# Plain-attention v as one stretch, key blocks of 128 under 160 queries, and half-height transposes in a windowed attention with a gated unit

## The chip, the cores and the metric

The kernel runs on one core of a Trainium2 chip. The metric is the device time of one launch in microseconds (us). The engines are TensorE (PE, matmuls; PEld is its weight loading), VectorE (DVE), ScalarE (ACT), GpSimd (POOL) and SyncE (SP), which here issues nearly all transfers.

## The reference, cut to what matters

```
q, k, v: (batch 8, heads 8, seq 576, head_dim 64), float32
rel = pos[:, None] - pos[None, :]
mask_plain = (rel >= 0) & (rel < 32)                        # heads 0 to 3
mask_dil   = (rel >= 0) & (rel < 128) & (rel % 4 == 0)      # heads 4 to 7
attn = softmax(where(mask, q @ k.T / 8, -1e9));  y = attn @ v
x = y, heads side by side: (8, 576, 512)
gate = sigmoid(causal depthwise convolution of x over 5 positions)
out = (gate * (x @ w_val)) @ w_out                          # (8, 576, 512) float32
```

Each query sees 32 keys: its own and the 31 before it (plain), or every fourth key of the last 128 (dilated).

## The kernel before, in words

A *unit* is four heads of one batch: the plain ones (0 to 3) or the dilated ones (4 to 7), so there are 16 units. In each batch but the last the dilated unit comes first. Per unit:

- `load_q` brings q and k as 128 partitions x 1152 values (576 KB each). v comes by `load_vd` (dilated: 80 and 112 partitions of 4 KB, 320 and 448 KB, overlapping in 48 rows of keys) or by `load_vp` (plain: two transfers of 64 partitions x 12 runs of 512 bytes, 384 KB each; the halves and blocks of 96 queries overlap by 32 keys).
- GpSimd casts the plain q and k to bf16 (`cvq`, `cvk`), and v (`cv`, line 325: dilated into `vd`, plain into `vpb`).
- `transposes` (line 469): 9 full 128x128 transposes for q and for k, into PSUM; `evict_t` copies them to `qT` and `kT` in two halves.
- `scores` (line 488): keys times queries. A plain task handles the even or the odd keys of two heads in blocks of 64 keys by 96 queries, 12 matmuls on 64x64 tiles of the array; a plain unit has four. A dilated task has 8 matmuls of 64 rows by 128 keys.
- `exps` (line 508, ACT) and `masks` (line 514, VectorE): 128 x 576 elements each, four per unit.
- `attn_p` (line 552): 24 matmuls of 64 rows and 65 columns (the 65th column of v is ones, and gives the softmax sum), two tasks per plain unit; `attn_d` (line 525) for the dilated units, into the same PSUM pair as its scores. `norm_p` and `norm_d` divide by the sum.
- `transpose_xp` (line 589: 12 of 96 columns per plain unit) and `transpose_xd` (line 573), and their evictions, write `xT`, a ring of three batches.

Per batch, once `xT` is complete: `conv` (line 607, 20 matmuls on 64x64 tiles for each of four channel chunks), `tanh` (ACT), `val` (line 622, 8 matmuls of 288 columns for each chunk) and `gate` (line 631, VectorE). The output: 36 tasks `outs` (line 638, 4 matmuls of 512 columns), `out_copy` into one of six `osb` buffers (line 643) and `store`.

The order of all this is made by the kernel's own planner when it is built. Each step is a `Task` with a key, a price in us for each engine that can take it, its dependences, its PSUM need (a *pair* of banks, a single *bank*, or a *score* pair, of which `SP` may be held at once) and, on PE, a shape class `cfg`: `F` full, `R` two row halves, `Q` quarters. `Plan` picks, at each step, among the tasks that can start within a slack of the earliest, the one with the lowest key; `KEY["W"]` is added for PE tasks of another shape than the current one, and `SWITCH` to their start. Where PE would stand idle early on, `fill` puts matmuls of `warm` (line 666). Transfers are issued by SP in one chain (`lane`), limited by `QUEUED` us of transfers on their way. The weights follow the loads of the unit that `WV` and `WO` name: units 0 and 1. The constants (identities, masks, `diag` for the convolution) are made mostly by GpSimd.

Of the kernel before, what the change touches and what calls it, by code (L numbers as in the profile page):

```python
# [1 line left out]

# [8 lines left out]
ALU = mybir.AluOpType  # L11


def hi_bf16(ap: bass.AP) -> bass.AP:
# [5 lines left out]
KEY = {"L": 171.6, "cv": -104.8, "T": -8.3, "ET": -139.2, "S": -21.7, "X": -137.2, "M": -69.8, "A": -31.3,  # L20
       "N": -35.2, "XT": 3.1, "XE": -124.1, "C": -15.3, "H": -46.4, "V": -4.0, "G": -205.2, "O":
       33.0, "P": -86.6, "SP": 2, "W": 10.4, "WV": 0, "WO": 1}


class Task:


    def __init__(self, name, key, opts, emit, deps=(), cfg=None, need=None,
                 frees=(), load=0.0, port=(), after=None, mm=0):
        self.name, self.key, self.opts, self.emit = name, key, opts, emit  # L30
        self.deps = [d for d in deps if d is not None]
        self.cfg, self.need, self.load, self.port = cfg, need, load, port
        self.frees = [f for f in frees if f is not None]
        self.after, self.mm = after, mm
        self.holders = 0
        for f in self.frees:
            f.holders += 1
        self.fin = None
        self.slot = None


class Plan:
# [6 lines left out]
    FETCH = 1.3  # L49
# [7 lines left out]
    def __init__(self, pairs, score_pairs):  # L57
# [6 lines left out]
        self.dma = 0.0  # L64
# [28 lines left out]
    def start_of(self, t, eng):  # L93
        s = self.free_at[eng]
        if eng == "PE" and t.cfg != self.cfg and self.cfg is not None:
            s += self.SWITCH
# [22 lines left out]
    def last_out(self, s, n):  # L119

        ahead = 0.0
        for d in reversed(self.queue[:n]):
            if d.start <= s:
                ahead += d.load
                if ahead > self.QUEUED:
                    return d
# [8 lines left out]
    def commit(self, t, eng, s):  # L135
# [5 lines left out]
        if t.load:  # L141
            self.dma = max(self.dma, s + (0.9 if t.name[0] == "s" else 2.4 if t.name[0] == "v" else 3.0)) + t.load
            t.fin = self.dma + 0.1
            if eng == "SP":
                t.start = s
                self.queue = sorted(self.queue + [t], key=lambda d: d.start)
        if eng in t.port:
            self.port[eng] = s + lat
        if eng == "PE":
            n = (self.mm + self.AHEAD) // self.LINE  # L150
            self.mm += t.mm
            for n in range(n + 1, (self.mm + self.AHEAD) // self.LINE + 1):
                self.dma = max(self.dma, s + 0.5) + self.FETCH
                self.lines[n + 1] = self.dma + 0.3
# [33 lines left out]
    def run(self):  # L188
# [12 lines left out]
        while ready:  # L201
            best = None
            for eng in self.free_at:
# [6 lines left out]
                s, k, t = min((x for x in c if x[0] <= s0 + self.SLACK[eng]), key=lambda x: (  # L210
# [11 lines left out]
        for n, t in enumerate(self.queue):  # L222
# [6 lines left out]
def kernel(  # L229
# [19 lines left out]
    QB = TT // 2  # L249
    KB = (80, 128)  # L250
    T1 = TT - KB[1]
    Z1 = 16
# [3 lines left out]
    NG = S // 192  # L256
# [5 lines left out]
    ETW = 400  # L262
# [7 lines left out]
    NVD, NQ, NE, NO = 3, 3, 6, 6  # L270
# [5 lines left out]
    qTs = [consts.tile([128, 2 * S], BF16, name=f"qT{i}") for i in range(2)]  # L276
    ets = [consts.tile([128, 2, ETW], BF16, name=f"et{i}") for i in range(NE)]
    vps = [consts.tile([128, 4 * NG, 2, D], FP32, name=f"vp{i}") for i in range(2)]
# [4 lines left out]
    vpb = [consts.tile([128, 2, 2 * NG, DA], BF16, name=f"vpb{i}") for i in range(NVD)]  # L283
# [4 lines left out]
    xnd = [consts.tile([QB, 8, 2, D], BF16, name=f"xnd{i}") for i in range(2)]  # L288
    xnp = [consts.tile([96, 2, NG, 2, 2, D], BF16, name=f"xnp{i}") for i in range(2)]
# [7 lines left out]
    ident_f = consts.tile([8, 8], FP32, name="ident_f")  # L297
    mask_d = consts.tile([128, HALF], BF16, name="mask_d")
    mask_p = consts.tile([128, 2, HALF], BF16, name="mask_p")
# [14 lines left out]

    def flat(ap):
# [12 lines left out]
    def band(dst, base, pattern, step):  # L328
        nc.gpsimd.affine_select(out=dst, in_=dst, compare_op=ALU.is_ge, fill=0.0,
                                base=base, pattern=pattern, channel_multiplier=-step)  # L330
        nc.gpsimd.affine_select(out=dst, in_=dst, compare_op=ALU.is_ge, fill=0.0,
                                base=W - 1 - base, pattern=[[-a, n] for a, n in pattern],
                                channel_multiplier=step)

    def eye(dst, n):
        nc.gpsimd.memset(dst, 0.0)
        nc.gpsimd.affine_select(
            out=dst, in_=dst, compare_op=ALU.not_equal, fill=1.0,
            base=0, pattern=[[-1, n]], channel_multiplier=1)

    def const(name, eng, dur, emit, deps=(), key=-50):
        return plan.add(name, key, {eng: (dur, dur + 0.05)}, lambda t: emit(), deps,
                        port=("POOL",))

    c_warm = const("warm0", "DVE", 0.5, lambda: nc.vector.memset(warm, 0.0), key=-60)  # L345
    c_eye = const("eye", "POOL", 1.0, lambda: eye(ident_b, 128), key=-60)
# [4 lines left out]
    c_sw = const("swap", "DVE", 0.25, swapped_eye, deps=[c_eye], key=5)  # L351

    def dil_mask():
        nc.gpsimd.memset(mask_d, 1.0)
        for z in range(2):
            band(mask_d[:, 2 * QB * z:2 * QB * (z + 1)].rearrange("p (h t) -> p h t", h=2),
                 z * (QB - T1), [[0, 2], [1, QB]], 1)

    c_md = const("mask_d", "POOL", 1.6, dil_mask, key=-57)

    def dil_ones():
        for x in vds[0] + vds[1] + vpb:
            nc.gpsimd.memset(x[:, :, :, D:DA], 1.0)
    c_vd = const("ones_d", "POOL", 0.4, dil_ones, key=-56)

    def small_eyes():
        eye(ident_f, 8)
        eye(ident_2[0:64], D)
        nc.gpsimd.tensor_copy(ident_2[64:128], ident_2[0:64])
    c_id = const("eyes", "POOL", 0.9, small_eyes, key=-55)  # L370

    def plain_mask():
        nc.gpsimd.memset(mask_p, 1.0)
        for s in range(2):
            m = mask_p[0:64, s, 0:96]
            nc.gpsimd.affine_select(out=m, in_=m, compare_op=ALU.is_ge, fill=0.0,
                                    base=W - s, pattern=[[1, 96]], channel_multiplier=-2)
            nc.gpsimd.affine_select(out=m, in_=m, compare_op=ALU.is_ge, fill=0.0,
                                    base=s - 1, pattern=[[-1, 96]], channel_multiplier=2)
        for g in range(1, NG):  # L380
            nc.gpsimd.tensor_copy(mask_p[0:64, :, 96 * g:96 * g + 96], mask_p[0:64, :, 0:96])
        nc.gpsimd.tensor_copy(mask_p[64:128], mask_p[0:64])
        nc.gpsimd.memset(mask_p[0:W // 2, :, 0:96], 0.0)
    c_mp = const("mask_p", "POOL", 2.6, plain_mask, key=-10)

    def dve_consts():
        for x in kTs:
            nc.vector.memset(x[:, 0:W], 0.0)
            nc.vector.memset(x[:, W + 2 * S:], 0.0)
        for x in ets:  # L390
            nc.vector.memset(x[:, :, HALF:], 1.0)
        nc.vector.memset(xT[:, :, :, 0:K - 1], 0.0)
        nc.vector.memset(vps[0][0:W // 2, 0], 0.0)
        for x in vas[1]:
            nc.vector.memset(x[0:Z1], 0.0)
    c_dv = const("dve_consts", "DVE", 2.2, dve_consts, key=-59)
# [8 lines left out]
    def dma(name, key, load, emit, deps=(), eng="SP", lane=None):  # L405
        def go(t):
            t.ins = emit()
            if getattr(t, "behind", None):
# [5 lines left out]
                     after=lane and lane[0])  # L414
# [19 lines left out]
    def load_vd(u, n, z):  # L434
        b = units[u][0]
        rows = v[b, 4:8].rearrange("h (p r) d -> p h (r d)", r=R)
        if z == 0:
            return [nc.sync.dma_start(out=vas[z][n % 2], in_=rows[0:KB[0]])]
        return [nc.sync.dma_start(out=vas[z][n % 2][Z1:KB[1]], in_=rows[T1 + Z1:TT])]

    def load_vp(u, n, half):
        b = units[u][0]
        dst = vps[n % 2][64 * half:64 * half + 64]
        first = v.offset + (b * H * S + 96 * half - W) * D
        skip = 1 if b == 0 and half == 0 else 0
        ins = []
        if skip:
            ins.append(nc.sync.dma_start(
                out=vps[n % 2][W // 2:64, 0].rearrange("p s d -> p (s d)"),
                in_=bass.AP(tensor=v.tensor, offset=v.offset,  # L450
                            ap=[[2 * D, 64 - W // 2], [1, 2 * D]])))
        ins.append(nc.sync.dma_start(
            out=dst[:, skip:].rearrange("p n s d -> p n (s d)"),
            in_=bass.AP(tensor=v.tensor, offset=first + skip * 192 * D,
                        ap=[[2 * D, 64], [192 * D, 4 * NG - skip], [1, 2 * D]])))
        return ins
# [4 lines left out]
    def transposes(t, u, name):  # L461
        d = units[u][1]
        if d:
            src = (qns if name == "q" else kns)[u % NQ]
        else:
            src = (qcs if name == "q" else kcs)[(u // 2) % 2]
        ps = pair(t).bitcast(BF16)
        for j in range(JP):
            nc.tensor.transpose(  # L469
                out=ps[:, j * 128:(j + 1) * 128],  # L470
                in_=hi_bf16(src)[:, j * 128:(j + 1) * 128] if d else flat(src[:, j]),
                identity=ident_b)

    def evict_t(t, tr, u, name, half):
        dst = kTs[u % 2][:, W:W + 2 * S] if name == "k" else qTs[u % 2]
        pv = pair(tr).bitcast(BF16)[:, 0:JP * 128].rearrange("p (j a) -> p a j", j=JP)
        dv = dst.rearrange("p (a j) -> p a j", j=JP)
        a = slice(64 * half, 64 * half + 64)
        copy(t, dv[:, a], pv[:, a])

    def scores(t, i, hf):
# [10 lines left out]
        if units[u][1]:  # L492
            for z in range(2):
                for hh in range(2):
                    o = (2 * e + hh) * 2 * TT + hf
                    for x in range(2):
                        mm(0, 128, (2 * z + hh) * QB, QB, x, W + o + 2 * z * T1, 2,
# [428 lines left out]
```

## Time and profile before

| what | value |
|---|---|
| three runs | 186.19, 186.78, 186.88 us; median 186.78 |
| the profiled execution | 189.71 us, of which the span of its instructions is 188.0 |
| mean granted clock of TensorE | 0.984 |
| transfers | 43.41 MB, mean 231 GB/s |
| fill matmuls of line 666 | 15.08 us of PE's busy time |
| Exp, 128 x 576 | 64 times, mean 654 ns |
| GpSimd idle, waiting for dilated v / plain v / k | 35.3 / 18.2 / 15.7 us |

The page is one execution taken by the hardware profiler. Its busy shares are means over the span; a stretch of the span can be asked for by itself, and so can the chain of waits that ended last, which is followed back from the last instruction. A group's row gives its line, engine, operation, tiles and shape, then the busy time and the mean of one in ns, then the idle time before it with what ended it. Matmuls are pipelined, so a group's mean is a latency and not the time that it takes from the next.

### The profile page before, as it was taken

The page shows a single profiled execution, that of the slowest core. Times are in us where ns is not written, and L with a number is a line of the kernel's source. Part 1 is how long each engine was busy: PE and PEld are TensorE (multiplying, and loading weights), DVE is VectorE, ACT ScalarE, POOL GpSimd, SP SyncE. Part 2 cuts the span into 40 slices and gives each one's busy share as a digit, 9 for nine tenths or more (in the row PEclk, how much of TensorE's full clock was granted, in tenths as well). Part 3 has the DMA queues.
Part 4 walks back from the last instruction along what each step waited for, and adds up shares of the span by engine and source line. Part 5 has one row for each costly group of instructions (what it writes and reads, how often), then busy time and mean ns, then how long its engine had stood idle before and what let it go on. Part 6 is the DMA issues. An engine that isn't in the chain of part 4 may idle for free.

```text
span 188.0 us, 6710 instructions
## 1 busy us (share of the span) xinstructions
PE 165.5 (88%) x2872; PEld 112.4 (60%) x2896; DVE 120.7 (64%) x233; ACT 124.3 (66%) x210; POOL 62.5 (33%) x99
## 2 busy tenths in 40 slices
PE   7988898998998999987998999789998999989930
PEld 2535455775685667664676677647676567557410
DVE  7498484795688858872877677567785488605000
ACT  2446799568775958684587846988777766672260
POOL 7974307325430723035153540711543230000000
PEclk9999999999999999996999999999999999999997
DMA  5999999899989988996799999859987840143265
GB/s 196 281 391 233 388 267 283 237 265 273 255 232 323 293 193 241 240 279 163 204 318 267 275 308 245 194 190 231 348 202 234 231 167 3 59 152 127 67 210 170
DMA packets 32102, 43.41 MB, mean 231 GB/s; under 512 B 1877, under 2 KB 20293, under 8 KB 32074
## 3 DMA queue, kind: packets, MB, share of 16 engines
q1 hardware_dynamic: 32064, 42.99, 80.7%
q8 instruction: 22, 0.36, 0.9%
q14 instruction: 6, 0.05, 0.1%
q10 hardware_dynamic: 10, 0.01, 0.0%
HBM read 33.56 MB, written 9.44 MB: 229 GB/s over the span
## 4 chain that ended last, share of the span: by engine, by line
PE 54%; DVE 12%; DMA 11%; ACT 11%; issue 6%; SPq 1%; ACTq 1%
PE ps L622 14%; PE ps L638 12%; PE ps L607 8%; PE ps L488 5%; PE ps L469 5%; DMA va<-in_v_dram 4%; ACT et L508 3%; DMA kn<-in_k_dram 3%; DVE et L514 3%; ACT osb L643 3%; DMA wst<-in_moe_w_out_dram 3%; PE ps L552 3%; PE ps L525 3%; DVE xnd L535 2%; PE ps L573 2%
## 5 line engine op out<-in xcount | busy, mean ns | idle before, releaser
L508 ACT ACTIVATE et<-ps 128x576 bf16<-128x576 f32 x64 | 40.6, 654 | 15.8 <-PE ps L488 14.6
L638 PE MATMUL ps<-w_out,gy 128*128 128x512 bf16 x125 | 34.0, 384 | 3.7 <-ACT osb L643 1.5
L622 PE MATMUL ps<-xT,w_val 128*128 128x288 bf16 x256 | 36.1, 287 | 0.6 <-DVE et L514 0.2
L325 POOL CAST vd<-va 80x512 bf16<-80x512 f32 (+1 forms) x32 | 19.3, 632 | 44.8 <-DMA va<-in_v_dram 35.3
L643 ACT ACTIVATE osb<-ps 128x512 f32<-128x512 f32 x36 | 20.8, 604 | 17.4 <-PE ps L638 11.4
L631 DVE SCALAR_TENSOR_TENSOR gy<-gy,ps 128x576 bf16<-128x576 bf16 x32 | 24.0, 750 | 12.6 <-PE ps L622 12.3
L622 PEld LDWEIGHTS <-w_val 128*128 128x128 bf16 x256 | 23.5, 97 | 8.3 <-issue 1.6
L607 PE MATMUL ps<-xT,diag 64*64 64x288 bf16 x640 | 24.6, 286 | 2.7 <-issue 1.8
L514 DVE TENSOR_TENSOR et<-et,mask_d 128x576 bf16<-128x576 bf16 x32 | 20.3, 640 | 8.7 <-ACT et L508 8.5
L615 ACT ACTIVATE gy<-ps 128x576 bf16<-128x576 f32 x32 | 20.4, 657 | 5.1 <-PE ps L607 4.6
L535 DVE TENSOR_TENSOR xnd<-ps,rec 72x512 bf16<-72x512 f32 x32 | 22.0, 687 | 1.1
L638 PEld LDWEIGHTS <-gy 128*128 128x128 bf16 x144 | 13.1, 99 | 15.5 <-issue 4.4
L325 POOL CAST vpb<-vp 128x768 bf16<-128x768 f32 x16 | 14.5, 935 | 22.3 <-DMA vp<-in_v_dram 18.2
L607 PEld LDWEIGHTS <-diag 64*64 64x64 bf16 x640 | 17.1, 106 | 6.7 <-issue 4.6
L488 PE MATMUL ps<-qT,kT 64*64 64x96 bf16 (+1 forms) x640 | 18.5, 205 | 1.8 <-ACT kT L323 1.1
L323 ACT COPY qT<-ps 128x576 bf16<-128x576 bf16 x26 | 15.7, 642 | 6.4 <-PE ps L469 5.6
L514 DVE TENSOR_TENSOR et<-et,mask_p 128x576 bf16<-128x576 bf16 x32 | 15.3, 493 | 6.0 <-ACT et L508 5.6
L488 PEld LDWEIGHTS <-kT 64*64 64x64 bf16 (+1 forms) x640 | 11.5, 102 | 12.8 <-issue 9.0
L323 ACT COPY kT<-ps 128x576 bf16<-128x576 bf16 x24 | 14.6, 646 | 4.1 <-PE ps L469 2.1
L666 PE MATMUL ps<-warm 128*128 128x512 bf16 x52 | 15.1, 415 | 2.4 <-DVE warm L345 1.3
L325 POOL CAST kc<-kn 128x1152 bf16<-128x1152 f32 x8 | 10.7, 1340 | 15.7 <-DMA kn<-in_k_dram 15.7
L323 ACT COPY xT<-ps 128x576 bf16<-128x576 bf16 (+1 forms) x19 | 13.6, 723 | 3.2 <-PE ps L638 2.0
(67 smaller groups left out, 179.2 us busy)
## 6 DMA issues: line engine op xcount, KB each, us to landing
qn<-in_q_dram SPq DMA_DIRECT2D x16, 576.0 KB, 5.4
kn<-in_k_dram SPq DMA_DIRECT2D x16, 576.0 KB, 6.9
out_dram<-osb SPq DMA_DIRECT2D x24, 256.0 KB, 3.2
vp<-in_v_dram SPq DMA_DIRECT2D x15, 384.0 KB, 6.0
va<-in_v_dram SPq DMA_DIRECT2D x8, 448.0 KB, 7.8
va<-in_v_dram SPq DMA_DIRECT2D x8, 320.0 KB, 7.0
out_dram<-osb SPq DMA_DIRECT2D x8, 192.0 KB, 2.3
wst<-in_moe_w_val_dram SPq DMA_DIRECT2D x2, 512.0 KB, 5.9
```

The source lines that it names most:

```text
L323: nc.scalar.copy(out=dst, in_=src)
L325: op(t.eng).tensor_copy(dst, src)
L488: nc.tensor.matmul(out=ps[po:po + pn, x, out_c:out_c + ln], lhsT=kw[rb, k0:k0 + (pn - 1) * kstep + 1:kstep], rhs=qT[rb, q0:q0 + (ln - 1) * ...
L508: nc.scalar.activation(out=ets[(2 * i + hf) % NE][:, :, 0:HALF], in_=ps[:, :, 0:HALF], func=AF.Exp, scale=scale)
L514: op(t.eng).tensor_tensor(out=ev, in0=ev, in1=m.to_broadcast([128, 2, HALF]), op=ALU.mult)
L535: nc.vector.tensor_tensor(out=xnd[i % 2][:, 4 * hf:4 * hf + 4].rearrange("p (x j) h d -> p x (j h) d", x=2), in0=av[:, :, :, 0:D], in1=rec ...
L607: nc.tensor.matmul(out=ps[o:o + 64, 512 * f:512 * f + HALF], lhsT=diag[lo:lo + 64, c * K + kk, :], rhs=xT[lo:lo + 64, b % NX, c, f * HALF ...
L615: nc.scalar.activation(out=gy[:, c, :, b, :], in_=ps[:, :, 0:HALF], func=AF.Tanh, scale=0.5)
L622: nc.tensor.matmul(out=ps[:, 512 * f:512 * f + HALF], lhsT=w_val[f][:, mc, c * 128:(c + 1) * 128], rhs=xT[:, b % NX, mc, K - 1 + f * HALF: ...
L631: nc.vector.scalar_tensor_tensor(out=y, in0=y, scalar=1.0, in1=ps[:, :, 0:HALF], op0=ALU.add, op1=ALU.mult)
L638: nc.tensor.matmul(out=ps, lhsT=y[:, c, 128 * n:128 * n + 128], rhs=w_out[f][:, c, :], start=(c == 0), stop=(c == NCH - 1))
L643: nc.scalar.activation(out=osb[z % NO], in_=bank(ou), func=AF.Copy, scale=0.5)
```

## The change

The plain v is loaded as one contiguous stretch of four heads: 1152 pairs of keys over 128 partitions, 9 pairs to a partition, in one transfer. The plain scores take two heads as one sequence of 18 blocks of 64 even and 64 odd keys (9 blocks a head), each seen by 160 queries: the 128 of its own positions and the 32 after. They go into three score tasks per unit instead of four, each 128 x 960, with their own Exp, mask and buffers (`etp`). The plain attention sums per block of 128 queries: two tasks of 35 matmuls. Its output transposes use column halves (class `Y`), 20 of 128 columns. The q and k transposes work on the two row halves (class `R`), 18 of 64 columns for each. The dilated v is loaded without overlap (80 and 64 partitions), and 32 of its rows are cast a second time into the second block; the dilated query blocks become 80 and 64 instead of 72 and 72, and the dilated attention takes a PSUM pair of its own. Masks, identities and `diag` are built mostly by VectorE. The planner gets a model of three transfer lanes, an order key for late outputs (`OB`), a tunable slack, new prices and new keys: w_val now follows unit 1 and w_out unit 2 (`WV` 1, `WO` 2), and three score pairs may be held.

```diff
-KEY = {"L": 171.6, ... "SP": 2, "W": 10.4, "WV": 0, "WO": 1}
+KEY = {"L": 336.6, ... "SP": 3, "W": -90.3, "WV": 1, "WO": 2, "OB": -5.9, "LOW": 0, "SL": 5.3}
...
-                s, k, t = min((x for x in c if x[0] <= s0 + self.SLACK[eng]), key=lambda x: (
+                s, k, t = min((x for x in c if x[0] <= s0 + (0.02 * KEY["SL"] if eng == "PE" else self.SLACK[eng])), key=lambda x: (
...
     def load_vd(u, n, z):
-        if z == 0:
-            return [nc.sync.dma_start(out=vas[z][n % 2], in_=rows[0:KB[0]])]
-        return [nc.sync.dma_start(out=vas[z][n % 2][Z1:KB[1]], in_=rows[T1 + Z1:TT])]
+        o = QB[0] * z
+        return [nc.sync.dma_start(out=vas[z][n % 2][o - T0[z]:o - T0[z] + QB[z]],
+                                  in_=rows[o:o + QB[z]])]
...
+    def load_vp(u, n):
+        b = units[u][0]
+        return [nc.sync.dma_start(
+            out=vps[n % 2].rearrange("p n s d -> p n (s d)"),
+            in_=bass.AP(tensor=v.tensor, offset=v.offset + b * H * S * D,
+                        ap=[[2 * D, 128], [256 * D, NP], [1, 2 * D]]))]
...
     def transposes(t, u, name):
         for j in range(JP):
-            nc.tensor.transpose(
-                out=ps[:, j * 128:(j + 1) * 128],
-                in_=hi_bf16(src)[:, j * 128:(j + 1) * 128] if d else flat(src[:, j]),
-                identity=ident_b)
+            for h in range(2):
+                a = slice(64 * h, 64 * h + 64)
+                ps = pair(t)[:, 512 * h:512 * h + 512].bitcast(BF16)
+                nc.tensor.transpose(out=ps[:, j * 64:(j + 1) * 64],
+                                    in_=src[a, j * 128:(j + 1) * 128], identity=ident_b[a, a])
...
+    def scores_p(t, u, g):
+        todo = [(n, x, half, x, 0, 64) for n in range(3) for half in range(2) for x in range(2)
+                if P_SLOT[g][x][n][0] != 4 or half == x]
+        if g == 2:
+            todo += [(2, x, 1 - x, 1 - x, p, 32) for p in (0, 32) for x in (1, 0)]
+        for n, bk, half, x, p, ln in todo:
+            nc.tensor.matmul(
+                out=ps[64 * half + p:64 * half + p + ln, c:c + QP],
+                lhsT=kw[rb, W + o + 2 * p + e:W + o + 2 * p + e + 2 * ln - 1:2],
+                rhs=qT[rb, o:o + QP], start=True, stop=True)
...
+    def attn_p(t, u, n, x):
+        for k in ks:
+            mm(k, 0, k, 0, 128, False)
+        mm(10 if x else 7, 0, 8 if x else 9, 0, 128, False)
+        for s in range(2):
+            for k in ks[:-1]:
+                mm(k, s, k + 1, 128, W, False)
+        for k in ks:
+            mm(k, 1, k, 0, 128, k >= ks[-2])
...
     def transpose_xp(t, u):
+            for n in range(5):
+                for e in range(2):
+                    nc.tensor.transpose(out=ps[64 * e:64 * e + 64, o:o + 128],
+                                        in_=xn[:, k % 2, k // 2 - 4 * x], identity=ident_b)
...
-    T_DG = add("diag", 4, {"POOL": (2.4, 2.5)}, lambda t: nc.gpsimd.tensor_tensor(
+    T_DG = add("diag", 4, {"DVE": (1.40, 1.45)}, lambda t: nc.vector.tensor_tensor(
...
-            TQ[u] = add(f"T{name}{u}", j0 + KEY["T"], {"PE": (0.50, 0.67)},
-                        [L[u] if d else C[u], c_eye], cfg="F", need="pair", mm=JP)
+            TQ[u] = [add(f"T{name}{u}", j0 + KEY["T"], {"PE": (0.31, 0.48)},
+                         (L[u] if d else [C[u]]) + dep + [c_eye], cfg="R", need="pair", mm=2 * JP)]
...
+                a = add(f"A{u}p{x}", j + KEY["A"], {"PE": (0.66, 0.83)},
+                        last + cvp[u][0:x + 1], cfg="R", need="pair", mm=35)
```

## The prediction

> **What bounds the kernel now.** I read the busy shares first, then the chain of waits, then the busy time by stretch, because a mean over the whole span hides that this kernel has three stages.
>
> ```profile
> PE 165.5 (88%) x2872; PEld 112.4 (60%) x2896; DVE 120.7 (64%) x233; ACT 124.3 (66%) x210; POOL 62.5 (33%) x99
> PE 54%; DVE 12%; DMA 11%; ACT 11%; issue 6%; SPq 1%; ACTq 1%
> ```
>
> TensorE (PE) is busiest and holds most of the chain that ended last. But 15.08 us of its 165.5 are the fill matmuls of line 666, which only keep it running: useful PE time is about 150 us. By stretch (columns: stretch, length, PE, PEld, DVE, ACT, POOL busy, clock, DMA share, GB/s):
>
> ```profile
> 0.00:30.00 30.00, 25.76 (x355) 14.50 (x361) 20.96 (x46) 18.62 (x30) 16.36 (x46) 1.00 0.99 293
> 30.00:150.00 120.00, 110.75 (x2185) 79.89 (x2200) 85.12 (x161) 87.58 (x150) 44.26 (x52) 0.99 0.92 251
> 150.00:180.50 30.50, 28.95 (x333) 17.99 (x336) 14.64 (x27) 15.88 (x27) 1.90 (x3) 1.00 0.30 98
> 180.50:188.00 7.50, 0.00 (x0) 0.00 (x0) 0.00 (x0) 2.26 (x5) 0.00 (x0) 0.82 0.60 204
> ```
>
> In the first 30 us the transfers run at 0.99 and 293 GB/s, and 14.48 of PE's 25.76 us are fills: the start is bound by loading. From 30 to 150 us PE is 92% busy and the transfers 92%: two limits lie side by side. After 150 us the loads are over and PE alone counts. After the last matmul, 7.5 us of copies and stores remain. The chain in order of time shows what the start waits for (columns: start, length, what):
>
> ```profile
> 2.28 7.35 DMA va<-in_v_dram
> 9.71 6.38 DMA kn<-in_k_dram
> 16.16 5.50 DMA wst<-in_moe_w_out_dram
> ...
> 33.25 0.98 PE ps L622 x8
> ```
>
> Three transfers in a row, the last one w_out, which no matmul needs until batch 0 is gated. The first value matmul starts at 33.25. Here the plain unit's k lands at 16.1 (9.71 + 6.38), behind q, k, v of unit 0 and the whole of w_val.
>
> **What the Trainium skill says.** "TensorEngine Tiling (Array Packing)", Key Properties: tiles of one mode load weights and multiply in parallel, and a change of mode drains the array. The trace agrees with both: the 24 plain attention matmuls of half height take 0.47 us in the chain, 19.6 ns each for 65 columns; and among 214 neighbouring pairs of groups in PE's timeline after 30 us, those of one shape overlap by 0.16 us, those of different shape (128 pairs) by 0.07, so a change costs 0.09 us. "SBUF — State Buffer", Who interferes with whom: a VectorE operation with two SBUF inputs and a GpSimd one that reads SBUF exclude each other. The trace agrees: the mask product has a median of 452 ns and a maximum of 3471 ns, in the start beside GpSimd's `diag` (2.32 us from 7.96). "ScalarE: Activation LUTs", What ACT_TABLE_LOAD costs: 186 ns + 0.833 ns per element for immediate scale and bias, 666 ns for 576 elements; measured 654.
>
> **The change part by part.** Durations are of the profiled execution: its own time is 189.71 us for a span of 188.0, against a median of 186.78. Some 2 us of the excess is one place, 83.8 us, where PE stands for 1.78 us at a dip of the clock (0.83 in 80 to 90 us). So I sum differences and apply them to the median.
>
> ```profile
> L488 PE MATMUL ps<-qT,kT 64*64 64x96 bf16 x384 | 9.4, 210 | 1.4 <-ACT kT L323 1.1 <-issue 0.3
> L552 PE MATMUL ps<-vpb,et 64*128 64x65 bf16 x384 | 9.0, 191 | 0.4 <-ACT et L508 0.4
> L589 PE MATMUL ps<-ident_b,xnp 96*128 96x96 bf16 x96 | 5.9, 216 | 0.1
> L469 PE MATMUL ps<-ident_b,qc 128*128 128x128 bf16 x72 | 5.3, 220 | 0.0
> ```
>
> The means are latencies of overlapped instructions; for a task's price I use its piece in the chain.
>
> 1. q/k transposes, 32 tasks: 9 full ones take 0.50 us; now 18 of half height and 64 columns. Nearest row: L552's 19.6 ns, so 18 x 19.6 = 0.35. Saving 0.15 x 32 = 4.7 us. Bounds: 0 if the halves don't overlap, 6 us if the planner's new price (0.31 for 0.50) is right.
> 2. Plain attention: 48 matmuls per unit become 70. 2 x 35 x 19.6 ns = 1.37 for 0.94 us: +0.43 x 8 = 3.5 us. Half of the 70 read or write less, so 2 to 3.5.
> 3. Plain scores: 48 of 96 columns become 38 of 160. A back-to-back task of 12 occupies 0.25 us with its change of shape (59.95 to 60.20). Four such run beside each other, so 64 more columns at TensorE's 128 columns in 55 ns (0.50/9) add 12/4 x 27 ns = 0.08. 3 x 0.33 + about 0.1 for the two extra = 1.09 against 4 x 0.25: +0.8 us over 8 units. Bounds 0 and 2.
> 4. Plain output transposes: 12 x 96 columns (0.51 us) become 20 x 128 on two column halves, which is 10 x 128 if they run together: +0.05 x 8 = 0.4 us; if not, +0.6 x 8 = 4.8. Line 607's 64x64 tiles run together, so I take 0.4. Dilated output transposes, 72 to 80 columns: 16 x 8 x 3.4 ns = 0.4 us.
> 5. So PE's own work is -4.7 + 3.5 + 0.8 + 0.4 + 0.4 = **+0.4 us**: nothing is won there.
> 6. Changes of shape: the q/k transposes become half-height, next to dilated scores and plain attention, but a new column shape appears and the bonus for staying in one shape, `KEY["W"]`, goes from +10.4 to -90.3, a reward for changing. Eight score tasks less could save 16 x 0.09 = 1.4; a third more changes costs 43 x 0.09 = 3.9. I take +1.2, bounds -1.4 and +9.
> 7. Transfers: plain v 2 x 384 KB becomes 576 KB, dilated v 768 KB becomes 576 KB, so 16 x 192 KB = **3.1 MB of 43.4** go. At 293 GB/s this is 10.7 us of transfer time, most of it behind PE. SP issues one plain v where it issued two (8 x 0.6 us); its longest waits are for ACT's copies, so I cost that at nothing. The contiguous source keeps 512-byte rows, so no rate gain is counted.
> 8. The start: with w_val behind unit 1 and w_out behind unit 2, unit 1's k has 2.95 MB ahead of or in it (q, k of two units, one v of 0.59 MB) instead of 4.18: 1.23 MB at 293 GB/s = **4.2 us earlier**. The constants that move to VectorE (`diag`, masks) free GpSimd and remove the 3.5 us mask product; w_val still lands before 18 us, well ahead of its first use. I take -4.2, bounds 0 and -6.
> 9. The middle: PE idles 9.25 us of 120, 2.06 of it in the disturbed stretch. With 0.39 MB per batch less (1.3 us of an 18.3 us batch) q, k and v land earlier. I take -2.2, a third of the 7.2 us; bounds +1 and -5. GpSimd, which now stands 35 us for `va`, gains from this too.
> 10. Elsewhere: Exp, 3 x 974 ns (654 + 384 x 0.833) for 4 x 654: +0.3 x 8 = 2.4 us on ACT, covered at 66% busy. Masks 3 x 0.75 for 4 x 0.45, norms 2 x 0.82 for 2 x 0.95: +1.5 us on VectorE, covered. Casts: plain 1152 elements for 1536, dilated six for four: about +6 us on GpSimd at 33%, part of it offered to VectorE and ACT. If the cover is gone, plain attention waits for all three masks of four heads at once (before: for two of two heads), and PE must have value or output matmuls to run in between; it has, except in the first and last unit. A dilated score pair is released after Exp instead of after its norm, while attention asks for its own: even. Tail: the stores' order changes; 0, bounds +1 and -1.5.
>
> Sum: +0.4 + 1.2 - 4.2 - 2.2 = **-4.8 us: 182.0 us**.
>
> **The rivals.** (a) *Everything sits behind PE*: the half-height transposes don't overlap (+4.7 on item 5), or the earlier start is only waited out later; the gains cancel and the time is about 186.7. For it: PE is 95% busy after 150 us. Against it: L552 overlaps. (b) *Loading was the true limit*: all of the 7.2 us idle in the middle goes, with the 4.2 of the start and the better end of items 1 and 6: about 176.5. For it: the 0.92 share. Against: most of PE's short waits are for ACT and VectorE, not transfers. (c) *Slower, by changes of shape*: the reward for changing breaks the runs of equal tasks between 30 and 180 us. At 0.09 us each, 71 more changes on the present 128 eat the 6.4 us of items 8 and 9; from there on it is slower. With 100 more (+9.0 for the +1.2 of item 6), the time is 186.78 + 0.4 + 9.0 - 6.4 = 189.8. For it: the key, and the slack of about 0.1 us is as large as the change. Against: with a change priced into a task's start, few candidates lie within it.
>
> **How the numbers follow.** A measurement of this kernel can tell about 0.5%, 0.93 us. Forecast 0.54 (own range 179.5 to 185), rival b 0.12, rival a 0.11, rival c 0.23. Faster: forecast and b, 0.66; same 0.11; slower 0.23. The range runs from rival b to rival c, 176.5 to 190.0; 0.1 lies outside on each side, mostly beyond the sizes of b and c.
>
> **What would show it.** Right: fills in the first 30 us well under 14 us and the first value matmul near 29 us; 18 half-height transposes in about 0.35 us; bytes near 40.3 MB; PE idle in the middle under 6%. Wrong: first value matmul still at 33, output transposes of 20 above 0.8 us, or the count of shape changes after 30 us near 200.

## The result, and the profile after

The changed kernel takes 198.7 us (197.09 to 199.11, 4 runs) against 186.83 in the same series: ratio 1.0631, 95% interval 1.0552 to 1.0711. It is **slower by 6%**, where 182.0 was forecast. Comparisons below use ratios to runs of the kernel before made beside them on the same chip, since chips differ (its median was 187.2 to 190.0 in the later series). The ratios leave out executions in the slower state that each kernel falls into now and then, so a ratio need not be the quotient of two medians.

The page after: busy shares, the clock and transfers by slice, packets, and the chain by engine.

```profile
span 197.4 us, 7613 instructions
PE 172.9 (88%) x3334; PEld 113.6 (58%) x3334; DVE 127.5 (65%) x256; ACT 126.7 (64%) x202; POOL 64.6 (33%) x90
...
PEclk9999589999999999997999999999999999999996
DMA  5999689987499556799287897960100030143785
...
DMA packets 27370, 40.34 MB, mean 204 GB/s; under 512 B 1733, under 2 KB 15557, under 8 KB 27338
...
PE 45%; DVE 16%; DMA 14%; ACT 10%; POOL 6%; issue 4%; SPq 1%; ACTq 0%; POOLq 0%; DVEq 0%
```

The 3.1 MB are gone, as forecast, and PE's share of the chain fell from 54 to 45%: more of the path is waits for others. There is a half-clock slice near 22 us and a dip near 90 us, and the transfers are nearly idle between 130 and 170 us and crowded at the end. By stretch (columns as before):

```profile
0.00:30.00 30.00, 25.14 (x404) 13.75 (x406) 19.97 (x69) 17.29 (x28) 15.75 (x30) 0.89 0.88 284
30.00:150.00 120.00, 108.34 (x2427) 76.40 (x2429) 90.88 (x158) 86.08 (x135) 48.83 (x61) 0.99 0.70 217
150.00:180.00 30.00, 29.18 (x472) 19.05 (x464) 16.68 (x31) 15.27 (x26) 0.00 (x0) 1.00 0.17 61
180.00:197.40 17.40, 10.28 (x47) 4.40 (x45) 0.00 (x0) 8.10 (x15) 0.00 (x0) 0.90 0.69 231
```

In the middle the DMA share fell from 0.92 to 0.70, and PE's busy time fell too, from 110.75 to 108.34: what the transfers gave up, PE did not take. VectorE rose from 85 to 91 us. After 180 us a new stretch has appeared in which PE still works and the stores run at 231 GB/s. What stands there is output work. The copies into `osb` by stretch (first two lines after: VectorE's and ACT's; the last two before, ACT's alone):

```profile
0.00:160.00 160.00, 3.45 (x5) 6.53 (x11) 0.97 0.69 217
180.00:197.40 17.40, 0.00 (x0) 8.10 (x15) 0.90 0.69 231
```

```profile
0.00:160.00 160.00, 13.73 (x23) 0.99 0.89 248
180.00:188.00 8.00, 2.56 (x5) 0.83 0.58 197
```

By 160 us the kernel before had copied 23 of 36 output blocks, the changed one 16. Its last gate ends at 177.1 us (before: 174.3), and when PE has done its last value matmul, a microsecond before that, 16 output tasks remain where 8 remained: 8 x 0.86 = 6.9 us of PE work, plus 1.1 us in which PE waits for ACT's copies, which wait for stores. So the last matmul ends at 191.4 instead of 180.4. The output task is unchanged; it is what PE had not got round to. The debt of some 10 us (6.9 and the 2.8 of the gate) was made before, in the start and the middle.

It is not idle time alone. Of the 11.0 us by which PE ends later, 7.4 are busy time (172.9 for 165.5) and 3.6 idle time (18.5 for 14.9, up to the last matmul). A part of the busy time is the clock: PE works 9.5 us at half clock (from 20 to 26.6 and from 88 to 91.5 us), in the kernel before 3.2 us (from 86 to 90). Half of the difference, some 3 us, can be put down to that; the other 4 us or so are more busy time at full clock.

### The profile page after: what moved, and what is told of

It is laid out like the page before. It is cut to its first block, busy times and chain, and to the rows that moved or that the text cites. A ratio compares the mean times of both kernels' runs of the same rounds, so it can differ in the third digit from the quotient of the medians.

```text
span 197.4 us, 7613 instructions
## 1 busy us (share of the span) xinstructions
PE 172.9 (88%) x3334; PEld 113.6 (58%) x3334; DVE 127.5 (65%) x256; ACT 126.7 (64%) x202; POOL 64.6 (33%) x90
## 2 busy tenths in 40 slices
DMA packets 27370, 40.34 MB, mean 204 GB/s; under 512 B 1733, under 2 KB 15557, under 8 KB 27338
## 4 chain that ended last, share of the span: by engine, by line
PE 45%; DVE 16%; DMA 14%; ACT 10%; POOL 6%; issue 4%; SPq 1%; ACTq 0%; POOLq 0%; DVEq 0%
PE ps L688 12%; PE ps L704 11%; PE ps L673 7%; DMA va<-in_v_dram 6%; DVE ep L560 5%; PE ps L609 5%; DMA vp<-in_v_dram 4%; POOL vd L340 4%; DMA out_dram<-osb 4%; PE ps L638 2%; ACT xT L338 2%; ACT osb L709 2%; PE ps L581 2%; PE ps L547 2%; DVE gy L697 2%
## 5 line engine op out<-in xcount | busy, mean ns | idle before, releaser
L340 POOL CAST vd<-va 96x512 bf16<-96x512 f32 (+2 forms) x45 | 29.9, 667 | 68.7 <-PE ps L581 34.6
L697 DVE SCALAR_TENSOR_TENSOR gy<-gy,ps 128x576 bf16<-128x576 bf16 x32 | 23.9, 751 | 14.6 <-PE ps L688 14.4
L688 PEld LDWEIGHTS <-w_val 128*128 128x128 bf16 x256 | 23.5, 99 | 10.4 <-issue 3.6
L709 ACT ACTIVATE osb<-ps 128x512 f32<-128x512 f32 x31 | 17.7, 599 | 13.1 <-PE ps L704 5.8
L560 DVE TENSOR_TENSOR ep<-ep,mask_p 128x960 bf16<-128x960 bf16 x24 | 22.4, 974 | 2.1 <-ACT ep L554 2.1
L564 ACT ACTIVATE et<-ps 128x576 bf16<-128x576 f32 x32 | 18.9, 667 | 7.2 <-PE ps L522 3.9
L554 ACT ACTIVATE ep<-ps 128x960 bf16<-128x960 f32 x24 | 21.7, 984 | 2.0 <-PE ps L547 2.0
L591 DVE TENSOR_TENSOR xnd<-ps,rec 80x512 bf16<-80x512 f32 x32 | 22.0, 687 | 1.1
L609 PE MATMUL ps<-vpb,ep 64*128 64x65 bf16 (+1 forms) x560 | 16.2, 197 | 2.9 <-DVE ep L560 2.5
L609 PEld LDWEIGHTS <-ep 64*128 64x128 bf16 (+1 forms) x560 | 12.0, 97 | 9.4 <-issue 3.2
L569 DVE TENSOR_TENSOR et<-et,mask_d 128x576 bf16<-128x576 bf16 x32 | 14.0, 469 | 5.2 <-ACT et L564 5.1
L581 PE MATMUL ps<-vd,et 96*128 96x65 bf16 (+1 forms) x256 | 12.7, 196 | 1.8 <-DVE et L569 1.1
```

The source lines that it names most:

```text
L340: op(t.eng).tensor_copy(dst, src)
L554: nc.scalar.activation(out=etp[(3 * n + g) % NEP][:, :, :, 0:QP], in_=ps.rearrange("p x (n c) -> p x n c", n=3), func=AF.Exp, scale=scale)
L560: op(t.eng).tensor_tensor(out=ev, in0=ev, in1=mask_p[:, g], op=ALU.mult)
L591: nc.vector.tensor_tensor(out=xnd[i % 2][:, 4 * hf:4 * hf + 4].rearrange("p (x j) h d -> p x (j h) d", x=2), in0=av[:, :, :, 0:D], in1=rec ...
L609: nc.tensor.matmul(out=ps[0:ln, o:o + DA], lhsT=etp[(3 * n + g) % NEP][rb, bk, m, c:c + ln], rhs=vb[rb, k // 2, s, :], start=out % 2 not i ...
L688: nc.tensor.matmul(out=ps[:, 512 * f:512 * f + HALF], lhsT=w_val[f][:, mc, c * 128:(c + 1) * 128], rhs=xT[:, b % NX, mc, K - 1 + f * HALF: ...
```

## The experiments

"Theory O" is that the order made from the new keys is slow; its rivals put the loss into the new steps (S), their masks (M), wrong prices in the planner (P), the clock (C) or the changes of shape (rival c).

**New keys, nothing else.** The planner's 24 keys were searched anew with the planner's own end as the measure.

```diff
-KEY = {"L": 336.6, ... "SP": 3, "W": -90.3, "WV": 1, "WO": 2, "OB": -5.9, "LOW": 0, "SL": 5.3}
+KEY = {"L": 893.6, ... "SP": 2, "W": -394.1, "WV": 0, "WO": 3, "OB": 285.7, "LOW": 0, "SL": 5.6}
```

> The changed kernel with other keys for the planner and nothing else: same steps, same prices. The planner's own end falls from 177.0 to 172.8 us. Theory O: the time falls by about as much or more, to 194.5 or less, and the order is what was slow. Theory S: the steps cost what they cost in any order, within 1.5 us of 198.7.

Measured: 189.01 us beside 187.18, ratio 1.0109 (1.0065 to 1.0153, 20 runs). About 5 of the 6.3% went with the order. "Order" is more than the sequence of tasks here: the new keys also put w_val back behind unit 0 and w_out behind unit 3 (`WV` 0, `WO` 3), and hold two score pairs. The page's first line, and its stretches:

```profile
PE 166.7 (90%) x3311; PEld 112.2 (60%) x3336; DVE 128.5 (69%) x260; ACT 125.7 (68%) x200; POOL 66.1 (36%) x88
30.00:150.00 120.00, 112.39 (x2512) 79.95 (x2526) 92.02 (x166) 91.56 (x145) 47.07 (x58) 1.00 0.72 227
180.00:186.00 6.00, 1.49 (x7) 0.58 (x6) 0.00 (x0) 1.45 (x3) 0.00 (x0) 0.83 0.63 221
```

The same steps, with the transfers at 0.72 (0.70 in the changed kernel), keep PE busy 4 us longer in the middle, at full clock, and leave 7 matmuls after 180 us. No half-clock stretch is left, and the first value matmul begins at 30.97 us instead of 33.22. Over the whole span PE's busy time falls by 6.2 us and its idle time before the last matmul by 3.7 (18.5 to 14.8). So a good part of what the order gives can be clock: half of the 9.5 us above.

**A second set of keys**, with 96 changes of shape where the first has 161.

> The changed kernel with a second set of keys, found from another starting point: planner's end 174.0 (172.8 for the first set), and 96 changes of shape on PE where the first has 161. Theory O (the planner's end tells the time): 1.2 us more than with the first set, a ratio of 1.013 to 1.025. Rival c (changes of shape decide, 65 x 0.09 = 5.9 us): below the first set, 0.98 to 0.99. If the first set was luck: 1.04 or more.

Measured: 1.0434 (1.0281 to 1.0587). Neither rival c nor the planner's end gave this; it is the size named beforehand for "the first set was luck". Its profile has the clock at half again, some 17 us of it (a clock of 0.66 from 12 to 27 us and 0.57 from 32 to 40):

```profile
PEclk9996588599999999999999999999999999999996
12.00:20.00 8.00, 4.94 (x89) 3.56 (x89) 4.34 (x11) 3.88 (x8) 4.56 (x6) 0.72 1.02 346
20.00:26.00 6.00, 5.15 (x96) 3.41 (x96) 5.03 (x9) 4.82 (x7) 2.64 (x4) 0.52 1.03 269
```

So 1.011 is a good order and not what any order gives. The two spans are 192.8 and 185.6 us; 14.4 us of PE's work at half clock could by itself be the 7.2 us between them.

**Rival c in one key.** `"W": -90.3` to `"W": 10.4` in the changed kernel.

> The changed kernel with KEY W at +10.4, its value before, and nothing else: the plan has 104 changes of array shape on PE for 160. Rival c of the prediction (changes of shape are the loss): 56 x 0.09 = 5.0 us faster, about 193.7. Theory O (the whole order counts; the planner's own end goes from 177.0 to 184.6): 203 or more.

Measured: 1.1089 (1.0977 to 1.1202). A third fewer changes of shape were planned, and it is slower by another 4 to 5%. But this profile has some 24 us at half clock (0.50 from 18 to 31 us, 0.57 from 96 to 100 and from 157 to 165) where the changed kernel has 10, so the run does not separate the two. Clearer is a count over the matmuls of the traces: after 30 us PE changes its array shape 185 times in the changed kernel (128 before) and 184 times with the first new keys. The same number of changes goes with 1.063 and with 1.011, so they are not what was lost between these two orders; both pay for them. The same key in the kernel before, `"W": 10.4` to `"W": -90.3`:

> The kernel before with KEY W at -90.3 and nothing else: 190 changes of shape for 141, planner's end 176.5 for 170.8. Theory O: 5.7 us or somewhat more, a ratio of 1.03 to 1.045. Rival c by its price alone: 49 x 0.09 = 4.4 us, 1.024. If the chip hides the changes: 1.01 or less.

Measured: 1.0452 (1.0098 to 1.0805): the sign is clear, the size is not. By the midpoint the old steps lose about as much by a foreign key as the new ones; the interval also holds the 1.024 of rival c's price.

**The weights later, alone**, in the kernel before: `"WV": 0, "WO": 1` to `"WV": 1, "WO": 2`.

> The kernel before with w_val behind unit 1 and w_out behind unit 2 (WV 1, WO 2) and nothing else. Item 8 of the prediction: k of unit 1 lands 4.2 us earlier and the time falls to about 183. Theory O (keys found for the other order of loads don't suit; the planner's own end goes from 170.8 to 177.8): 192 or more.

Measured: 1.0333 (1.0184 to 1.0482). Item 8 had the wrong sign when the other keys stay. In the changed kernel this move was never undone alone, and it is an open rival to the rest of the order: its three sets of keys with `WV` 1 are at 1.043, 1.063 and 1.109, the three with `WV` 0 (the first new keys and the two runs with other prices, below) at 1.011, 1.028 and 1.035.

**The masks.** What plain attention waits for, in the chain of the changed kernel (start, length, what), and the mask's group:

```profile
60.46 0.97 ACT ep L554
61.44 0.02 issue
61.46 0.93 DVE ep L560
62.39 0.67 DVE gy L697
63.05 2.51 DVE ep L560 x2
```

```profile
L560 DVE TENSOR_TENSOR ep<-ep,mask_p 128x960 bf16<-128x960 bf16 x24 | 22.4, 974 | 2.1 <-ACT ep L554 2.1
```

Three masks, with a gate between, take 4 us during which GpSimd casts (its line stands at 59.92 to 67.8 us without a break). The mask's minimum is 643 ns, its median 741, its maximum 1606. The experiment halves it:

```diff
-        ev = etp[(3 * n + g) % NEP][:, :, :, 0:QP]
-        op(t.eng).tensor_tensor(out=ev, in0=ev, in1=mask_p[:, g], op=ALU.mult)
+        ev = etp[(3 * n + g) % NEP][:, :, :, 0:QP // 2]
+        op(t.eng).tensor_tensor(out=ev, in0=ev, in1=mask_p[:, g, :, :, 0:QP // 2], op=ALU.mult)
```

> The changed kernel in its own order, but each plain mask product works on half of its elements (the other keys stay unmasked). A mask falls from 0.93 to about 0.5 us, 24 x 0.43 = 10 us of VectorE. Theory M (the long masks, three in a row for all four heads and lengthened by GpSimd's casts, are what plain attention waits for): 3 us or more go, 195.5 or less. Theory O: under 1 us, 197.7 or more.

Measured: 193.57 us beside 187.18, 1.034 by the medians (no interval was given): about 5 us less than the changed kernel's ratio. The masks are on the path in this order. A part of it is clock again: in the changed kernel PE stands 1.44 us for a mask before 85.45 us and has the clock at half from 88 to 91.5; with halved masks that stretch is gone (clock 1.00 from 30 to 150 us).

**The clock.** Stretches of the changed kernel, then of the one with more fills:

```profile
12.00:20.00 8.00, 5.13 (x102) 2.91 (x102) 4.35 (x11) 4.82 (x8) 4.56 (x6) 0.99 1.03 356
20.00:26.00 6.00, 5.27 (x79) 2.94 (x73) 4.68 (x8) 3.77 (x7) 2.27 (x4) 0.50 0.63 157
```

```profile
12.00:20.00 8.00, 5.98 (x110) 3.33 (x107) 4.35 (x11) 3.97 (x7) 4.56 (x6) 1.00 0.94 311
20.00:26.00 6.00, 5.27 (x114) 3.08 (x105) 3.85 (x8) 4.65 (x8) 0.72 (x2) 1.00 0.92 223
```

```diff
-        while a + self.GAP < b:
-            d = Task("fill", 0, {}, self.idle)
+        while a + (0.1 if 12 < a < 20 else self.GAP) < b:
+            d = Task("fill", 0, {}, (lambda t: [self.idle(t) for _ in range(4 if 13.2 < t.start < 14 else 2)])
+                     if 12 < a < 20 else self.idle)
```

> The changed kernel in its own order, with ten more fill matmuls on the early part of PE's order (12 to 20 us of the plan), where PE stood 2.9 us of 8 in 12 to 20 us and was then granted half the clock for 6 to 7 us. Theory C (the idle start costs the clock): the half-clock stretch goes and with it some 3 us, about 195.5. Theory O alone (the early stretch waits for GpSimd and ACT at any clock): within 1 us of 198.7.

Measured: 1.0467 (1.0276 to 1.0657), some 3 us below 1.0631 by the midpoints, and no half-clock stretch is left, the one at 88 us included. The interval still holds 1.0631, so the size is not settled. Between 12 and 20 us PE of the changed kernel had stood 2.0 us for VectorE and 0.8 us for GpSimd's cast of q, which the planned fills did not cover.

**The 32-column matmuls.** Groups of the changed kernel (rows*columns of the array tile, then shapes):

```profile
L609 PE MATMUL ps<-vpb,ep 64*128 64x65 bf16 x304 | 11.3, 197 | 2.9 <-DVE ep L560 2.5 <-DVE qT L340 0.4
L609 PE MATMUL ps<-vpb,ep 64*32 64x65 bf16 x256 | 7.1, 197 | 0.0
```

Each attention task goes from 64*128 to 64*32 and back. The edit makes them one shape:

```diff
+            if ln == W:
+                c, ln, out = QP - 128, 128, k
```

> The changed kernel in its own order, but the 32-column matmuls of the plain attention (256 of its 560) read 128 columns and add into their own block, so the task keeps one array shape; that part of the attention is computed wrongly, the work is otherwise the same. Theory S (the new steps themselves cost more than the old): a task of 35 falls from 0.86 to 0.69 us, as the two changes inside it go, and 16 x 0.17 = 2.8 us of that reaches the end: about 195.9 for 198.7. Theory O (the order made from the new keys is what is slow, PE waits in it for other engines): the task falls as far, but at most 1 us reaches the end: 197.7 or more.

Measured: 1.0437 (1.031 to 1.0565). In the chain a task of 35 goes from 0.86 to 0.66:

```profile
69.45 0.86 PE ps L609 x35
```

```profile
102.35 0.65 PE ps L611 x35
```

So 0.10 us for each change, 16 x 0.20 = 3.2 us. By the midpoints some 3.6 us reach the end, as theory S says (2.8) and not theory O (1 at most); the two intervals just touch. The same edit with the new keys:

> The changed kernel with the new keys (ratio 1.011 to the kernel before), and the 32-column matmuls of plain attention reading 128 columns into their own block, so that the tasks keep one shape (that part of the attention is computed wrongly). In a better order PE's own work should count: theory S gives the whole 16 x 0.17 = 2.8 us, a ratio near 0.996. Theory O (still waits): under 1 us, 1.006 or more.

Measured: 1.0016 (0.9898 to 1.0133), beside 1.0109. The direction fits, the interval covers both theories.

**The transposes**, undone with the new keys: 9 of 128 columns into one run of PSUM, as in the kernel before.

> The changed kernel with the new keys, but the q and k transposes full again (9 of 128 columns), in the same order. Item 1 says that the halves save 0.15 us each, 26 of 32 behind the start: undoing them costs 3.9 us, a ratio near 1.032. If the saving never reached the end: within 1 us, 1.006 to 1.016.

Measured: 1.0204 (1.0124 to 1.0284) beside 1.0109: about 1.8 of the 3.9 us by the midpoints, between the two outcomes named and with intervals that overlap. The halves alone in the kernel before, with the loop of the change's `transposes` and its two banks:

> The kernel before in its own order, with the q and k transposes on row halves alone (18 of 64 columns, two PSUM banks). Item 1 of the prediction: 0.15 us for each task, 26 of 32 behind the start, 3.9 us faster if PE is what counts: about 183. If the gain is swallowed by waits or by changes of shape (up to 64 x 0.09 = 5.8): 186 to 188.

Measured: 1.016 (1.0041 to 1.0279), slower than both outcomes named, with the clock at 0.56 from 18 to 25 us. With more fills, the edit shown above:

> The kernel before with the row-half transposes alone, as before (ratio 1.016, with a half-clock stretch at 18 to 25 us), and with more fill matmuls from 12 to 20 us of the plan. If the clock was the loss: the stretch goes, and the ratio falls to 1.00 or, with item 1's gain coming through, to 0.98. If the fixed order makes the gain a wait: 1.01 or more.

Measured: 1.0208 (0.9979 to 1.0438). The half-clock stretch goes and the time does not follow; with so wide an interval this settles only that no gain appears in the old order.

**The transfers alone**, in the kernel before: `skip` is 3 blocks for later plain units and the later dilated loads begin at partition 64.

> The kernel before in its own order, with v loaded without the overlapping rows from the third unit of each kind on: 2.36 MB less of 43.4 (old rows stay in their place, so attention is computed from wrong values there). Item 9 and rival b (transfers are a limit in the middle): 1.7 us faster or more, ratio 0.991 or less. If the transfers are covered: within 0.7 us, 0.996 to 1.004.

Measured: 1.0082 (0.9967 to 1.0198). The DMA share in the middle falls from 0.92 to 0.83 and nothing is gained in this order; the 0.991 of item 9 lies below the interval.

**Prices that hold on the chip.** `{"PE": (0.66, 0.83)}` to `(0.77, 0.94)` for plain attention, `{"DVE": (0.61, 0.67)}` to `(0.80, 0.88)` for its mask, keys searched anew:

> The changed kernel with two prices of the planner set to what the chip showed (plain attention 0.77 for 0.66, plain mask 0.80 for 0.61) and keys searched anew for these prices. Theory P (wrong prices make PE wait in its fixed order): below the kernel with new keys alone, 187 or less. Theory O without P (any well searched order does): 188 to 191.

Measured: 1.0282 (1.0151 to 1.0412). With the mask at 0.66 and doubled fills:

> The changed kernel with plain attention priced at 0.77 and the plain mask at 0.66 (its time when GpSimd is quiet), keys searched for these prices (planner's end 174.6), and every fill matmul from 12 to 26 us of the plan doubled. Theory P (prices that hold on the chip, and the clock kept): a ratio of 1.005 or less, the first version below or at the kernel before. Without P: 1.01 to 1.03.

Measured: 1.0352 (1.0221 to 1.0484). Neither passes the first new keys, so better prices did not lead the search to a better order. As two searches with the same prices are 3% apart, that does not clear the prices. This second profile has 5 us at half clock after PE stood 2.3 of 5 us. No version was found that passes the kernel before.

## Why the prediction was wrong, point by point

The forecast summed costs of steps and gave 6.4 us of gain to a start and a middle whose order it could not see. That failed, in **items 8 and 9 and the cover claimed in item 10**: no gain came at the start, the middle idles more, and the masks are waited for. The clock, for which no item allows, lost some 3 us more by the count above. Of the prices of the steps, **item 2** was mis-sized by 2.7 us; the others held fairly well.

1. Transposes: 0.35 us forecast, 0.37 measured in the chain. The price was right; by the midpoints about half of the saving reached the end in the good order, none in the old one.
2. Plain attention: 0.69 forecast, 0.86 measured. The term was mis-sized: 32-column outputs were counted as cheaper or equal, and they are another array shape. The 0.09 us a change of item 6 was in hand; it was not applied inside a task. This costs 3.2 us of PE, where "2 to 3.5" had been allowed for the whole item, which came to 16 x 0.86 less 16 x 0.47 = 6.2.
3. Plain scores: 0.80 us for the 38 matmuls in one run (77.47 in the chain; the median distance to the next task is 0.96) instead of 1.09; better than forecast. Item 4: 0.68 where 0.51 had become 0.56, so 1.4 us instead of 0.4.
5. PE's own work was forecast as even, and it is so within some us. With the trace's median distances between starts, (0.37 - 0.60) x 32 for the transposes, (0.86 - 0.48) x 16 for attention, about -1 for the scores and +0.8 for the output transposes make -1.5 us. The 0.60 holds changes of shape and waits, though: with the chain's 0.50, 0.47 and 0.51 for the old tasks it is about +2. PE's whole busy time agrees better with the latter: 166.7 us in the good order at full clock, 165.5 in the kernel before with 3.2 us of it at half clock. So work is a small part of the loss.
6. Changes of shape, and with them **rival c**: its sign was right, its size (up to 190.0) too small, and its mechanism is not the main one. The changes did rise, from 128 to 185 after 30 us, near the 200 named as a sign of being wrong; 35 of these lie inside tasks and are in the prices of items 2 and 3, and 22 more between tasks are 2.0 us at 0.09, for 1.2 forecast. But the good order has 184.
7. The bytes fell to 40.34 MB as forecast. That they matter was wrong: bytes taken from the kernel before alone shortened nothing, which also speaks against **rival b**. (Its own terms give about 173 and not 176.5: 186.8 + 0.4 - 1.3 - 1.4 - 4.2 - 7.2.)
8. The start: the first value matmul begins at 33.22 us (before: 33.09). k did land early: GpSimd casts it at 14.29 without waiting for it (before: 16.15), and PE transposes it 3.5 us earlier. Plain attention, which follows, begins 2.2 us later all the same. PE in the changed kernel, then in the kernel before:

```profile
15.49 0.44 PE L503 MATMUL ps<-ident_b,kc 64*128 64x64 bf16 x18
17.02 1.16 PE L581 MATMUL ps<-vd,et 96*128 96x65 bf16 x24 [1.10 <-DVE et L569]
25.80 1.24 PE L609 MATMUL ps<-vpb,ep 64*128 64x65 bf16 x35
```

```profile
12.87 0.79 PE L525 MATMUL ps<-vd,et 80*128 80x65 bf16 x16 [0.64 <-DVE et L514]
19.01 0.68 PE L469 MATMUL ps<-ident_b,kc 128*128 128x128 bf16 x9
23.64 0.66 PE L552 MATMUL ps<-vpb,et 64*128 64x65 bf16 x24
```

What comes late is the dilated attention (17.02 for 12.87), for which PE waits. In the chain of the changed kernel:

```profile
8.32 1.48 POOL vd L340
...
13.20 1.16 POOL qc L340
14.40 0.46 PE ps L503 x18
```

Six casts of dilated v run from 8.32 to 13.1, then q's cast, and only then PE can transpose q of the plain unit. That is earlier than before (15.26). But VectorE has the copy of this q in front of the dilated masks:

```profile
15.55 0.76 DVE L340 COPY qT<-ps 128x576 bf16<-128x576 bf16 x1 [5.64 <-ACT qT L338]
16.22 1.86 DVE L569 TENSOR_TENSOR et<-et,mask_d 128x576 bf16<-128x576 bf16 x4
```

ACT ends the four Exp for these masks at 12.42; VectorE stands 5.64 us for the copy first. PE's scattered waits here come before the half clock of 20 to 26.6 us. The forecast asked when the data lands and not what is queued in front of its first readers. Moving `diag` could not free the 3.5 us mask either: that mask ran from 9.34 to 12.8 us in the kernel before, `diag` ended at 10.28, and GpSimd's casts of dilated v ran from 10.23 to 12.5.

9. The middle: PE idles 11.7 us of 120 instead of the 7 expected (before: 9.25). (The 2.2 us was called a third of 7.2, which is 2.4.)
10. VectorE was called covered at 64%. Plain attention now needs all three masks, they come in a row, and GpSimd's casts stretch the mean to 974 ns for 750. Item 10 named this wait and then trusted that value or output matmuls stand between. PE waits 2.5 us for masks in the middle, 1.44 of it at 84 us. By 85 us two batches were gated, which are 9 output blocks, and 8 output tasks had run: at most one was left to fill in.

What the single edits gave (keys 5%, masks about 3%, clock and shape about 1.5 to 2% each) is not a sum: they overlap. Shown is that another order of the same steps, the order of the weights' loads included, takes about 5 of the 6.3%. That this is because the new keys were not fitted to the new steps is an argument, not a measurement: the planner's own end supports it (177.0 us, 172.8 after a search, 170.8 for the kernel before), and so do the two edits of keys that hurt the kernel before. It stays open how much of the 5% is the place of the weights alone, how much the clock and how much the waits; whether a longer search would bring the changed steps below the kernel before; and why the second set of keys, 1.2 us apart in the plan, is 3% apart on the chip, for which the half clock may be enough.

The signs named in advance: transposes and bytes came out right. The fills (13.05 us in the first 30, before 14.48) fell a little, not "well". The first value matmul, PE's idle time (9.7%) and the count of changes came out on the wrong side; the 20 output transposes (0.68 us) stayed below the 0.8 that would have been a sign of being wrong.

## What to carry to other kernels

In a kernel whose engines follow one fixed order, price the order before the steps: for each new or moved step ask what is queued ahead of it on the engine that reads it first, and let no share of 64% stand for "covered" where three such steps must all end before the next engine starts. Ask the planner first: its own end, each kernel at its own prices, was 177.0 us for 170.8, a loss of 6 us where the sum of the steps promised 4.8 of gain, and over the four sets of keys of the changed kernel at its own prices (172.8, 174.0, 177.0, 184.6) the measured ratio rises with it (1.011, 1.043, 1.063, 1.109). It is a rough guide: the two edits of the kernel before stand the other way round (176.5 and 1.045, 177.8 and 1.033, with intervals that overlap). Freed bandwidth is worth nothing if PE does not wait for transfers. Work left over at the end, here 16 output tasks for 8, is the place where the waits of the whole kernel are paid.

## What the runs showed of the hardware

- The granted clock fell to 0.50 for nearly 7 us (20 to 26.6) after PE had worked 5.13 of 8 us, with no single wait above 1.1 us; with more fills, 5.98 of 8 us, it stayed at 1.00. The Trainium skill, "TensorE: Matmul & The Clock Gate", What's actually happening, gives half the clock after an idle window of about 3.4 us; the half agrees, but here scattered waits were enough.
- A change of array shape inside a task costs 0.10 us also when only the columns change (64*128 to 64*32), in line with the drain that "TensorEngine Tiling (Array Packing)", Key Properties, states.
- A mask of two SBUF inputs takes 643 ns at its shortest (two in 1.21 us at 150.33, after GpSimd's last cast) and up to 1606 ns; two of them at 62.98, beside GpSimd's casts, took 2.58 us.
